# Sums of x, the first group's second half, quarter sums and stores of results moved in a kernel of sliding-window attention and Sinkhorn-routed experts

## The chip, the cores and the metric

The kernel runs on one core of one Trainium2 chip. The metric is the device time of one execution in microseconds (us). The engines are called as the profile calls them: PE (TensorE matmuls), PEld (its weight loads), DVE (VectorE), ACT (ScalarE), POOL (GpSimd) and SP (SyncE, which here only issues transfers). Each engine runs its own instructions in the order of the program and waits on semaphores for the others.

## The reference

Attention over 8 batches, 8 heads, 576 positions of 64, in a window of 128 back, with a bias that falls linearly with the distance. Its output, 4608 tokens of 512, is the input `x` of a mixture of 8 experts: all experts work on all tokens, and the routing weights come from 8 rounds of Sinkhorn normalisation over all tokens.

```python
def _attn_ref(q, k, v):
    ...
    mask = (rel >= 0) & (rel < window)
    scores = np.where(mask, scores + bias[None], -1000000000.0)
    ...
    return np.matmul(attn, v)

def _moe_ref(x, w_gate, w1, w2):
    ...
    P = np.exp(logits)
    for _ in range(8):
        P /= P.sum(1, keepdims=True) + 1e-09
        P /= P.sum(0, keepdims=True) + 1e-09
        P *= N / E
    out = np.zeros((N, D), dtype=np.float32)
    for e in range(E):
        h = np.maximum(x @ w1[e], 0.0)
        ye = h @ w2[e]
        out += P[:, e:e + 1] * ye
    return out
```

## The kernel before

The order of every engine's instructions is written out by hand in the program: what is called first is issued first.

**The attention stage** runs over 8 batches, each in 5 blocks of keys (`kb`, four of 128 and a tail of 64) and two halves of the heads (`u`). A step `(b, kb, u)` has a place in its batch, `at = 2 * kb + u`. A step issues the scores of the step ahead on PE (L412, L419), its exponentials on ACT (L430), the mask on DVE (L443), the products with v of the present step on PE (L468), and their normalisation on DVE (L478, L479). Around this stands what prepares the coming batches:

- `load_qk` (L271) loads q and k of batch b + 2 at `at == 3`, through SP's queue.
- `cast_qk` casts them to 16 bits in four parts: k on ACT (L289), q on DVE (L287). The first two parts of batch b + 2 are cast at places 8 and 9 of batch b, the others at places 0 and 1 of batch b + 1. On ACT the first of them stands ahead of the exponentials of batch b + 1.
- `turn_qk` (L301) turns q and k of batch b + 1 with two transposing transfers in SP's queue, at `at == 1`, for b = 2 to 6. `order_qk` (L312) brings them into order, k on POOL and q on DVE.
- `turn_x` writes the turned attention output into the tiles `xT`, from batch 3 on with a transposing transfer (L519).

**The filler** puts the dense products of experts 0 and 1 between these steps, so that PE has work while the softmax chain is under way: `l1` (L115, eight 128x512 products and a ReLU on ACT, L127) and `l2` (L137, eight matmuls into one bank, then `keep`). `keep` casts the result on DVE into a tile `yo` (L555); the tiles rotate through `YO` slots. The cast result isn't stored at once. It is appended to a list, and `store(left)` (L541) issues the stores of all but the last `left` of the list, in order, on SP's queue; `keep` calls `store(2)` ahead of its cast. A cast into a slot that is used again waits until the store from that slot has landed. The PSUM banks of the tag `pmm` are four, shared by the products of the filler, the attention and the units below; a bank is free when the cast or copy that reads it is done.

**The Sinkhorn rounds** follow, with filler between.

**The routed stage** handles experts 2 to 7. A unit is a group of 256 tokens and an expert, 108 units in order of group, `n` counts them. Most units make both products with seven partial products in place of eight (Strassen's scheme). This needs sums of quarters of the operands: for `x` the function `sums_x` (L909 to L911, three DVE instructions), for the first weights `quads_w1` (L933, four per expert; for expert 7 one of them is split in two, L931), for the second weights `sums_of` (L630, five per expert). The last two are put into a list `todo`, and `some(k)` issues the next k of them; `more_sums` says how many unit n issues near its beginning and at its end. Units of experts 6 and 7 of the first group (n = 4, 5) use plain products (`l1_bank`, L957), since their quarter sums aren't made yet.

In a seven-product unit, PE's banks go by letters: product A, a copy of A into B on ACT (L1138), product C, a copy of C into the tile `s5y` (L1142), more onto B, a copy of B into C (L1147), and so on. L1153 and L1159 are the two DVE additions that end the first layer's unit; the next product into bank B waits for L1153. `make_sums` (L995 to L997) adds up the hidden activations, and `product` (L1015) makes the second layer of the unit before, in between. When a group ends, `gather` (L1059) adds the banks into `acc` on DVE, which frees them for the next group.

`begin(g, e)` puts the stored results of experts 0 and 1 into `acc`: the first half L1031, the second L1035. They are loaded by `load_y` (L1025). For the first group the second half's load is issued at the end of unit 4, and `begin(g, 1)` stands near the beginning of unit 5, ahead of unit 5's `sums_x` for unit 6.

The passage between the stages runs so: x of the first two units is scaled and transposed (L887, L897), then the last filler products go in pieces, with some quarter sums after each:

```python
        got = filler.fill(0.9)
        some(int(got / L1_US + 0.5))
        got = filler.fill(0.9)
        sums_x(0)
        while got:
            some(int(got / L1_US + 0.5))
            got = filler.fill(0.9)
```

Of the kernel before, what the change touches and what calls it, by code (L numbers as in the profile page):

```python
# [14 lines left out]
def kernel(  # L15
# [18 lines left out]
    E = moe_w_gate.shape[1]  # L34
# [129 lines left out]
            yield 0, a  # L164

    L1_US, L2_US = 0.87, 1.74
    XPE, YO, XSB = 3, 6, 12
    CAST_AT = ((0, 1, 2, 3), (1, 2, 3, 4))

    class Filler:  # L170
# [58 lines left out]
    if True:  # L229
# [308 lines left out]
        def store(left=0):  # L538
            while len(stores) > left:
                e, blk, yo = stores.pop(0)  # L540
                nc.sync.dma_start(out=ysp[e, blk], in_=yo)  # L541
# [101 lines left out]
        def some(n):  # L643
            for _ in range(min(n, len(todo))):
                todo.pop(0)()
# [43 lines left out]
        for n, (b, kb, u) in enumerate(steps):  # L689
            nxt = steps[n + 1] if n + 1 < len(steps) else None  # L690
            at = 2 * kb + u
            left = ((10 - at) % 10 + 1) if b >= XPE else 10 - at + 9 * (at == 9)
            budget = filler.backlog() / (11 if (b, at) == (XPE, 0) else left)
            if b == 0:
                budget = 0.0
            if nxt:
                if nxt[0] < XPE and nxt[1:] == (RI - 2, 1):
                    turn_pe(nxt[0], 0, NDT)
                if nxt == (1, 0, 0):
                    filler.ready = RI  # L700
                    spin_alone(6)
                    for _ in range(NFT):
                        filler.take()
                    cast_qk(1, 0)
                    cast_qk(1, 1)
                    for j in range(NDT):
                        turn_pe(1, 1, j)
                        turn_pe(1, 0, j)
                        if j < 2:
                            cast_qk(1, j + 2, (1,))  # L710
                        filler.take()
                if nxt == (2, 0, 0):
                    filler.fill(8.5)
                    cast_qk(2, 0)
                    cast_qk(2, 1)
                    filler.fill(2.5)
                    for j in range(NDT):
                        turn_pe(2, 1, j)
                        turn_pe(2, 0, j)
                        if j < 2:  # L720
                            cast_qk(2, j + 2, (1,))
                        filler.fill(1.0)
                if n == 0:
                    scores(*nxt)
                elif nxt[2] == 0:
                    scores(*nxt)
                    scores(*nxt[:2], 1)
                exps(*nxt)
            got = filler.fill(1.0) if b else 0.0
            if nxt:  # L730
                masks(*nxt)
            values(b, kb, u)
            if n > 0 and u == 0 and by_pe(steps[n - 1][0]):
                turn_x(*steps[n - 1][:2])
            if u == 1 and n // 2 + NKB < B * NKB:
                cast_v(n // 2 + NKB)
            filler.fill(budget - got)
            if at == 0 and b > XPE:
                filler.ready = 4 * b
            if at < 8 and b < XPE:  # L740
                filler.ready = 4 * b + at // 2
            if at == 8 and b < XPE:
                filler.ready = 4 * b + 4
            if u == 1 and not by_pe(b):
                turn_x(b, kb)
            if u == 1:
                if kb == 1 and b > 0:
                    gates(4 * b - 4, 4 * b)
                if n // 2 + NKB + 1 < B * NKB:
                    load_v(n // 2 + NKB + 1)  # L750
            if b == 0 and at == 5:
                load_weights(1)
            if (b, at) == (1, 8):
                filler.allowed.add(1)
            if (b, at) == (1, 5):
                for j in (2, 3):
                    cast_qk(2, j, (0,), True)
            if (b, at) == (1, 2):
                filler.hold = False
            if (b, at) == (0, 9):  # L760
                load_qk(2, 2)
            if (b, at) == (0, 7):
                homes(1)
            if (b, at) == (1, 3):
                homes(2)
            if 1 <= b < B - 2 and at == 3:
                load_qk(b + 2)
            if XPE <= b + 1 < B - 1 and at >= 8:
                cast_qk(b + 2, at - 8)
            if XPE <= b + 1 < B:  # L770
                if at == 0 and b + 1 == XPE:
                    cast_qk(b + 1, 0)
                    cast_qk(b + 1, 1)
                if at < 2:
                    cast_qk(b + 1, at + 2)
                if at == 1:
                    turn_qk(b + 1)
                    order_qk(b + 1, 1, range(NDT))
                if at == 5:
                    turn_tail(b + 1)  # L780
                if at in (6, 7):
                    order_qk(b + 1, 0, range(2 * at - 12, 2 * at - 10))
            if b < B - 1 and at == (1 if b > 1 else 5) and b:
                load_tail(b + 1)
            if 10 * b + at >= 66:
                i = 10 * b + at - 66
                if i % 8 == 0:
                    home_last(2 + i // 8)
                (load_w2 if i % 8 < 4 else load_w1)(2 + i // 8, i % 4, 4)
            if (b, at) == (7, 0):  # L790
                todo += sums_of(2, *extras(2))
            if b == 7 and at >= 5:
                some(1)
# [302 lines left out]
        for e in range(2, 5):  # L1096
            todo += quads_w1(e)
        todo += quads_w1(5)
        got = filler.fill(0.9)
        some(int(got / L1_US + 0.5))  # L1100
        got = filler.fill(0.9)
        sums_x(0)
        while got:
            some(int(got / L1_US + 0.5))
            got = filler.fill(0.9)
        todo += sums_of(5, *extras(5))
        store()
# [2 lines left out]
        todo += sums_of(6, F1_6, w2f[:, 2], w2f[:, 3])  # L1110
        todo += sums_of(7, aux[:, 0], w2f[:, 0], w2f[:, 1]) + quads_w1(6) + quads_w1(7)
        more_sums = {0: (0, 1), 1: (2, 1), 2: (2, 1), 3: (2, 0), 4: (2, 1), 5: (2, 1), 6: (2, 0)}
        more_sums.update({n: (2, 0) for n in range(7, 11)})
        s5y = per.tile([P, 2, GT], FP32, name="s5y", tag="xTt", bufs=1)
        s5 = s5y[:, 0].rearrange("p (f t) -> p f t", f=NF2)
        y = s5y[:, 1].bitcast(FP16).rearrange("p (m d) -> p m d", m=2)
# [2 lines left out]
        for n in range(N):  # L1119
            g = units[n - 1][0]  # L1120
# [4 lines left out]
            some(more_sums.get(n, (0, 0))[0])  # L1125
            if done:
                gather(units[n - 2][0], 6, 7)
            if n > 0 and units[n - 1][1] == 6:
                begin(g, 1)
            y_first_half = n > 0 and units[n - 1][1] == (5 if g == groups[0] else 4)  # L1130
            if y_first_half:
# [1 line left out]
            if strassen(n):  # L1133
                new_h(n)
                pa = bank(n, "A")
                part(n, pa, "a11", B11, True)
                pb = bank(n, "B")
                nc.scalar.copy(out=pb, in_=pa)  # L1138
                product(n - 1, 3)
                pc = bank(n, "C")  # L1140
                part(n, pc, "s1", T1, True)
                nc.scalar.copy(out=s5, in_=pc)  # L1142
                product(n - 1, 4)
                if end:
                    gather(g, 3, 4)
                part(n, pb, "s2", T2)
                nc.scalar.copy(out=pc, in_=pb)  # L1147
                part(n, pa, "a12", B21)
                relu(n, 0, pa)
                scale_x(n + 2)  # L1150
                product(n - 1, 5, 2)
                part(n, pb, "s3", T3)
                nc.vector.tensor_tensor(out=h[n][:, 3], in0=pb, in1=s5, op=ALU.add)  # L1153
                relu(n, 3, h[n][:, 3])
                if done:
                    gather(units[n - 2][0], 1)
                part(n, pc, "s4", B22)
                turn_xs(n + 2)
                nc.vector.tensor_tensor(out=h[n][:, 1], in0=pc, in1=s5, op=ALU.add)  # L1159
                relu(n, 1, h[n][:, 1])  # L1160
                sums_x(n + 1)
                if end:
                    gather(g, 5, 2)
                product(n - 1, 6, 7)
                part(n, pb, "a22", T4)
                relu(n, 2, pb)
                product(n - 1, 1)
            else:
                pairs = ((3, 4), (5, 2), (6, 7), (1,))
                for i in range(4):  # L1170
                    l1_bank(n, i)
                    if i == 1:
                        scale_x(n + 2)
                    product(n - 1, *pairs[i])
                    if end and i in (0, 1):
                        gather(g, *pairs[i])
                turn_xs(n + 2)
                sums_x(n + 1)
            some(more_sums.get(n, (0, 0))[1])
            if done:  # L1180
                finish(units[n - 2][0])
# [42 lines left out]
```

## Time and profile before

| | us |
|---|---|
| median of 3 runs | 1018.19 (1016.83 to 1020.91) |
| the profiled execution | 1019.14 |
| its span, first to last instruction | 1017.4 |
| DVE busy | 754.7 |
| ACT busy | 728.9 |
| mean granted clock of PE | 0.998 |

The profile records one execution. Its views group instructions by source line, list them in order of time with the idle time of the engine before each and what ended that idle time, and sum busy times over stretches. A wait for several events is put down to the last of them. The attention stage takes up to about 280 us, the Sinkhorn rounds and the passage up to about 340, and the rest is the routed stage. The span starts at 0.

### The profile page before, as it was taken

Reading aid. Unit: us, or ns where it says so; the run is one execution under the profiler, and the core shown is the slowest. Engines: PE = TensorE matmul, PEld = TensorE weight load, DVE = VectorE, ACT = ScalarE, POOL = GpSimd, SP = SyncE. Lnnn points to the kernel's source line nnn. Section 1 sums busy time; section 2 is a strip of 40 time slices with the busy share of each in tenths; the row PEclk is TensorE's granted clock in tenths of the full one; section 3 lists DMA queues with packets and bytes.
Section 4 is the critical chain, followed back from the end, with each engine's and each line's share of the span. In section 5 each row is a group of like instructions: output and inputs, shape, how many; then the busy total and the mean of one; then the engine's idle time right before and its main releaser. Section 6 shows DMA issues by size and latency. Waiting matters only on the chain.

```text
span 1017.4 us, 27990 instructions
## 1 busy us (share of the span) xinstructions
PE 999.1 (98%) x11583; PEld 803.1 (79%) x11583; DVE 754.7 (74%) x1614; ACT 728.9 (72%) x1252; POOL 78.1 (8%) x143
## 2 busy tenths in 40 slices
PE   8999999999999999999999999999999999999998
PEld 5645444444444698999999999999999999999997
DVE  5837565655677979877877877887887887787787
ACT  7655554555333667888888888888888888888885
POOL 1213123315110000000000000000000000000000
PEclk9999999999999999999999999999999999999999
DMA  9998799889998223334333334334334333433461
GB/s 251 206 252 216 146 210 234 210 185 170 231 191 171 69 63 87 69 77 95 78 65 99 74 65 95 74 64 96 80 63 98 82 74 78 94 74 66 98 113 50
DMA packets 264431, 122.46 MB, mean 120 GB/s; under 512 B 201968, under 2 KB 255728, under 8 KB 264304
## 3 DMA queue, kind: packets, MB, share of 16 engines
q1 hardware_dynamic: 249568, 102.68, 44.3%
q0 software_dynamic: 14304, 17.84, 10.6%
q8 instruction: 90, 1.47, 0.6%
q14 instruction: 37, 0.30, 0.1%
q10 hardware_dynamic: 432, 0.16, 0.1%
HBM read 78.30 MB, written 23.59 MB: 100 GB/s over the span
## 4 chain that ended last, share of the span: by engine, by line
PE 86%; DVE 4%; DMA 4%; SPq 3%; issue 1%; ACT 1%; POOL 0%; DVEq 0%; POOLq 0%; ACTq 0%
PE psM L1015 31%; PE psB L978 14%; PE psh L115 9%; PE psA L978 9%; PE psC L978 9%; PE psy L137 9%; PE psN L468 1%; DMA ysp<-yo 1%; PE psS L412 1%; SPq L271 1%; DMA v<-in_v_dram 1%; DMA k<-in_k_dram 1%; PE psh L957 1%; SPq L374 1%; DVE yo L555 1%
## 5 line engine op out<-in xcount | busy, mean ns | idle before, releaser
L1015 PEld LDWEIGHTS <-hs 128*128 128x128 f16 x2996 | 271.1, 98 | 23.6 <-issue 1.6
L1015 PE MATMUL psM<-w2l,hs 128*128 128x256 f16 x1440 | 186.6, 273 | 1.0 <-DVE acc L1059 1.0
L978 PEld LDWEIGHTS <-w1l 128*128 128x128 f16 x2848 | 181.3, 98 | 5.8 <-issue 1.6
L991 ACT ACTIVATE hs<-hs 128x512 f16<-128x512 f16 x212 | 130.5, 631 | 35.0 <-DVE hs L1153 25.0
L978 PEld LDWEIGHTS <-s 128*128 128x128 f16 x2136 | 141.6, 98 | 7.7 <-issue 1.7
L1153 DVE TENSOR_TENSOR hs<-psB,s5y 128x512 f16<-128x512 f32 x106 | 73.3, 692 | 98.2 <-ACT xs L887 91.6
L115 PE MATMUL psh<-xT,w1t 128*128 128x512 f16 (+1 forms) x608 | 140.3, 371 | 3.3 <-DVE yo L555 2.1
L127 ACT ACTIVATE hT<-psh 128x512 f16<-128x512 f32 (+1 forms) x144 | 83.2, 587 | 82.2 <-PE psh L115 82.0
L887 ACT ACTIVATE xs<-xtok,L_sb 128x512 f16<-128x512 f16 x204 | 136.5, 723 | 2.7 <-DMA xset<-xs 2.7
L137 PE MATMUL psy<-w2t,hT 128*128 128x512 f16 x576 | 135.0, 379 | 0.0
L1015 PE MATMUL psM<-more,hs 128*128 128x256 f16 x864 | 129.4, 273 | 0.0
L978 PE MATMUL psB<-xset,s 128*128 128x128 f16 x1424 | 108.5, 219 | 0.4 <-ACT psC L1147 0.4
L978 PE MATMUL psA<-xset,w1l 128*128 128x128 f16 x1424 | 108.5, 219 | 0.0
L137 PEld LDWEIGHTS <-hT 128*128 128x128 f16 x576 | 53.5, 98 | 60.3 <-issue 1.9
L115 PEld LDWEIGHTS <-w1t 128*128 128x128 f16 x608 | 55.0, 99 | 56.5 <-issue 8.1
L430 ACT ACTIVATE pt<-psS 128x1024 f16<-128x1024 f32 (+2 forms) x80 | 67.7, 852 | 43.5 <-PE psS L419 20.0
L555 DVE CAST yo<-psy 128x512 f16<-128x512 f32 x68 | 46.7, 690 | 69.8 <-PE psy L137 53.8
L995 DVE TENSOR_TENSOR hs<-hs 128x1024 f16<-128x1024 f16 x107 | 74.0, 691 | 21.3 <-ACT hs L991 19.3
L1147 ACT COPY psC<-psB 128x512 f32<-128x512 f32 x106 | 60.5, 571 | 37.7 <-PE psB L978 37.7
L1142 ACT COPY s5y<-psC 128x512 f32<-128x512 f32 x106 | 62.2, 587 | 22.3 <-PE psC L978 22.2
L1138 ACT COPY psB<-psA 128x512 f32<-128x512 f32 x106 | 61.0, 575 | 23.4 <-PE psA L978 23.3
L1059 DVE TENSOR_TENSOR acc<-acc,psM 128x256 f32<-128x256 f32 (+1 forms) x162 | 73.9, 503 | 0.3
(121 smaller groups left out, 1385.3 us busy)
## 6 DMA issues: line engine op xcount, KB each, us to landing
s5y<-ysp SPq DMA_DIRECT2D x36, 256.0 KB, 3.0
ysp<-yo SPq DMA_DIRECT2D x68, 128.0 KB, 3.6
v<-in_v_dram SPq DMA_DIRECT2D x32, 256.0 KB, 4.7
out_dram<-acc SPq DMA_DIRECT2D x31, 256.0 KB, 2.6
q<-in_q_dram SPq DMA_DIRECT2D x5, 1024.0 KB, 7.4
k<-in_k_dram SPq DMA_DIRECT2D x5, 1024.0 KB, 9.9
xtok<-xd SPq DMA_DIRECT2D x34, 128.0 KB, 2.3
w2t<-in_moe_w_dram POOLq DMA_DIRECT2D x4, 1024.0 KB, 10.5
```

The source lines that it names most:

```text
L115: nc.tensor.matmul(out=ps[:, 0:nt], lhsT=w1ts[e][:, dt, P * ft : P * ft + P], rhs=xT[:, at : at + nb, dt, :], start=(dt == 0), stop=(dt == ...
L127: nc.scalar.activation(out=st["hT"][:, ft, 0:nt], in_=ps[:, 0:nt], func=AF.Relu)
L137: nc.tensor.matmul(out=ps, lhsT=st["hT"][:, ft, P * ms : P * ms + P], rhs=w2ts[e][:, ft, :], start=(ft == 0), stop=(ft == NFT - 1),)
L430: nc.scalar.activation(out=pt[0:nk, :, 0 : nk + nn], in_=ps[0:nk, :, :, 0 : nk + nn].rearrange("p a y n -> p (a y) n"), func=AF.Exp, scale ...
L887: nc.scalar.mul(out=xs[2 * (n % 2) + m], in_=xtok[m], mul=P_sb[:, blk, e : e + 1])
L978: nc.tensor.matmul(out=ps[:, j, :], lhsT=q[k][:, P * j : P * j + P], rhs=xset[n % 2][:, x, P * k : P * k + P], start=(start and j == 0 and ...
L991: nc.scalar.activation(out=h[n][:, slot], in_=src, func=AF.Relu)
L995: nc.vector.tensor_tensor(out=t[:, 4:6], in0=t[:, 0:2], in1=t[:, 2:4], op=ALU.add)
L1015: nc.tensor.matmul(out=Ms[bk][:, half, :], lhsT=h[n][:, LEFT[m], f, :], rhs=W2L[e][RIGHT[m]][:, f, :], start=(e == 2 and f == 0 and half = ...
L1059: nc.vector.tensor_tensor(out=a, in0=a, in1=p2, op=op)
L1142: nc.scalar.copy(out=s5, in_=pc)
L1153: nc.vector.tensor_tensor(out=h[n][:, 3], in0=pb, in1=s5, op=ALU.add)
```

## The change

Four things move, and one count grows:

1. `YO` is 7 in place of 6: one more slot for the cast results.
2. `store(1)` is called ahead of `turn_qk` in batches 2 to 6: all stores on the list but the last are issued ahead of the two transposes. On SP's queue these are two stores each time, which stood behind the transposes before.
3. `sums_x(0)` stands after the eighth piece of the last filler work, not after the second. On DVE it moves behind eight instructions that make quarter sums and one cast of a result.
4. The first group's `begin(g, 1)` moves from near the beginning of unit 5 to its end, behind `sums_x(6)`.
5. The quarter sums of experts 6 and 7 that unit 7 issued (two) are issued from unit 8 on, some at the ends of units 8 and 9.

The instructions of PE, ACT and POOL, and their order, stay as they are.

```diff
-    XPE, YO, XSB = 3, 6, 12
+    XPE, YO, XSB = 3, 7, 12
...
                 if at == 1:
+                    store(1)
                     turn_qk(b + 1)
...
         todo += quads_w1(5)
+        pieces = 0
         got = filler.fill(0.9)
-        some(int(got / L1_US + 0.5))
-        got = filler.fill(0.9)
-        sums_x(0)
         while got:
             some(int(got / L1_US + 0.5))
+            pieces += 1
+            if pieces == 8:
+                sums_x(0)
             got = filler.fill(0.9)
...
-        more_sums.update({n: (2, 0) for n in range(7, 11)})
+        more_sums.update({8: (2, 1), 9: (2, 1), 10: (2, 0)})
...
-            if n > 0 and units[n - 1][1] == 6:
+            if n > 0 and units[n - 1][1] == 6 and g != groups[0]:
                 begin(g, 1)
...
                 sums_x(n + 1)
+            if n == E - 3:
+                begin(g, 1)
             some(more_sums.get(n, (0, 0))[1])
```

## The prediction

> **What bounds the kernel now.** First the page's head, then the busy time in stretches of 25 us (columns: stretch and its length, then busy time and instructions of PE, PEld, DVE, ACT, POOL, the granted clock, DMA share, GB/s).
>
> ```profile
> span 1017.4 us, 27990 instructions
> PE 999.1 (98%) x11583; PEld 803.1 (79%) x11583; DVE 754.7 (74%) x1614; ACT 728.9 (72%) x1252; POOL 78.1 (8%) x143
> ```
>
> ```profile
> 125.00:150.00 25.00, 22.91 (x164) 10.87 (x160) 15.16 (x35) 13.77 (x23) 7.95 (x13) 0.93 0.88 212
> 325.00:350.00 25.00, 22.11 (x189) 14.10 (x188) 20.14 (x37) 14.46 (x26) 0.00 (x0) 1.00 0.28 70
> 375.00:400.00 25.00, 23.16 (x308) 21.53 (x306) 23.87 (x49) 17.46 (x32) 0.00 (x0) 1.00 0.31 76
> ```
>
> TensorE bounds the kernel: 18.3 us of the span is all that it idles. The change leaves TensorE's instructions and their order as they are, so it can win only idle time of PE and time at a lowered clock. The three stretches shown idle 2.1, 2.9 and 1.8 us, and in the first the mean clock is 0.93, worth up to 25 x 0.07 = 1.75 us. These are the three places that the change touches, so 8.5 us is a ceiling.
>
> **Place A, the entry into the first seven-product unit.** VectorE and PE, from the timeline (start, length, engine, line; the idle time before, in brackets):
>
> ```profile
> 331.40 0.43 DVE L909 TENSOR_TENSOR xset<-xset 128x512 f16<-128x512 f16 x1 [3.21 <-DMA xset<-xset]
> 332.25 7.07 PE L137 MATMUL psy<-w2t,hT 128*128 128x512 f16 x32
> 332.47 1.28 DVE L933 TENSOR_TENSOR s<-w1l 128x1024 f16<-128x1024 f16 x2
> 336.20 0.69 DVE L555 CAST yo<-psy 128x512 f16<-128x512 f32 x1
> 340.67 0.61 PE L978 MATMUL psC<-xset,s 128*128 128x128 f16 x8 [0.90 <-DVE yo L555]
> 343.66 0.68 DVE L1153 TENSOR_TENSOR hs<-psB,s5y 128x512 f16<-128x512 f32 x1
> 344.40 0.61 PE L978 MATMUL psB<-xset,w1l 128*128 128x128 f16 x8 [0.79 <-DVE hs L1153]
> ```
>
> VectorE stands 3.21 us for the transposes of x, is then late with four casts of finished sums (yo), and PE waits for their banks and for L1153. The change puts the three sums of x (332.47 - 331.40 = 1.07 us) behind eight quarter sums and one cast. The 3.21 us then fill with quarter sums. What is late next is the data of the first yo cast: it needs the first 8 of PE's 32 matmuls, 332.25 + 7.07/4 = 334.0, while the old queue reached it at 336.20. From 334.0 on the queue is the old one with 1.07 us of sums inside, so every later VectorE step moves by 336.20 - 334.03 - 1.07 = 1.10 us: the cast that frees psC's bank, and L1153. PE's gap at 340.67 closes, and its restart at 344.40, set by L1153, moves by 1.10. I take **-1.1 us**. The ends: 0.4 (the copies on ScalarE between the products set the pace instead) and 0.90 + 0.79 = 1.7 (both gaps gone). The moved sums end near 337.0 and are first read by psC, near 339.6: 2.6 us of cover; without it PE would pay their delay one for one. Up to the cast that frees psC's bank, one cast and two quarter sums queue behind them; the 1.10 already holds that.
>
> **Place B, the end of the first group.**
>
> ```profile
> 369.76 2.50 SPq L897 DMA_TRANSPOSE xset<-xs  x2
> 375.29 1.42 DVE L1035 SCALAR_TENSOR_TENSOR acc<-s5y,L_sb,acc 128x512 f32<-128x512 f16 x2 [1.98 <-DMA s5y<-ysp]
> 376.62 0.42 DVE L909 TENSOR_TENSOR xset<-xset 128x512 f16<-128x512 f16 x1
> 377.61 0.68 DVE L630 TENSOR_TENSOR w2f<-w2t 128x1024 f16<-128x1024 f16 x1
> 378.34 0.60 PE L1015 MATMUL psM<-w2f,hs 128*128 128x256 f16 x4 [0.34 <-DVE w2f L630]
> 383.01 0.61 PE L978 MATMUL psB<-xset,w1l 128*128 128x128 f16 x8 [0.54 <-DVE hs L1153]
> 387.45 1.28 DVE L933 TENSOR_TENSOR aux<-w1l 128x1024 f16<-128x1024 f16 x2
> 388.65 0.74 DVE L1059 TENSOR_TENSOR acc<-acc,psM 128x256 f32<-128x256 f32 x2
> 389.45 1.03 PE L1015 MATMUL psM<-w2l,hs 128*128 128x256 f16 x8 [0.97 <-DVE acc L1059]
> ```
>
> L1035 (the second half's begin) waits 1.98 us for its load, with the sums of x queued behind it. The change runs the sums first. Their transposes were issued at 369.76, ahead of that load in the same queue, so they should have landed by then. So 377.61 - 376.62 = 0.99 us of work goes into the wait, and the quarter sum w2f, then L1153, come 1.0 us earlier. That removes the gap of 0.34 and most of that of 0.54. The gap of 0.97 falls because the two quarter sums at 387.45 (388.65 - 387.45 = 1.20) no longer stand ahead of the gather at 388.65 that frees PE's bank. The idle times sum to 1.85. The first two are worth at most the 1.0 by which VectorE moves. For the third I add the 0.17 by which a group of 8 (0.61 busy) outlasts its share of the pace (32 matmuls of four times the width in 7.07: 0.055 each, 0.44 for 8): 1.1. I take **-2.1 us**, ends 1.0 (only the third) and 2.3 (all three with their tails).
>
> The quarter sums that leave unit 7 land in units 8 to 10, one more at the end of 8 (0.60) and two halves at the end of 9:
>
> ```profile
> 397.93 0.69 DVE L995 TENSOR_TENSOR hs<-hs 128x1024 f16<-128x1024 f16 x1 [0.20 <-ACT hs L991]
> 401.66 0.68 DVE L1153 TENSOR_TENSOR hs<-psB,s5y 128x512 f16<-128x512 f32 x1
> 402.69 0.61 PE L978 MATMUL psB<-xset,w1l 128*128 128x128 f16 x8
> ```
>
> In unit 9 L1153 ends at 402.34 and PE needs it at 402.69: 0.35 us of cover, against about 0.3 of delay (the 0.60, less a 0.2 us wait that it fills and a shorter first half). I cost it at nothing; uncovered it is 0.3 us, once.
>
> **Place C, the stores ahead of the transposes of q and k.** The timeline of batch 3, and the clock in three windows of 2 us:
>
> ```profile
> 117.77 6.27 SPq L301 DMA_TRANSPOSE qk<-c  x2
> 125.44 1.64 SPq L541 DMA_DIRECT2D ysp<-yo  x3
> 128.46 0.69 DVE L555 CAST yo<-psy 128x512 f16<-128x512 f32 x1 [4.22 <-DMA ysp<-yo]
> 129.20 1.86 PE L115 MATMUL psh<-xT,w1t 128*128 128x512 f16 x4 [2.09 <-DVE yo L555]
> ```
>
> ```profile
> 128.00:130.00 2.00, 0.80 (x2) 0.25 (x2) 1.54 (x3) 0.45 (x1) 2.00 (x3) 0.80 0.71 184
> 130.00:132.00 2.00, 2.00 (x13) 1.03 (x12) 1.33 (x5) 0.60 (x1) 0.45 (x2) 0.50 0.88 179
> 132.00:134.00 2.00, 2.00 (x15) 0.76 (x13) 1.62 (x3) 0.72 (x2) 1.53 (x3) 0.85 0.85 282
> ```
>
> The stores of results stand on SP's queue behind 6.27 us of transposes; a cast waits 4.22 us for its slot, PE 2.09 for the cast, and then runs at half clock for 0.8 + 2.0 + 0.6 = 3.4 us, a loss of 1.7. Either edit alone removes this wait: two stores go ahead, and with seven slots a cast waits for the store seven before it instead of six. So 3.8 us vanish at 129.2. But PE has the next wait in sight:
>
> ```profile
> 130.25 0.89 SPq L271 DMA_DIRECT2D k<-in_k_dram  x1
> 140.85 0.62 ACT L289 CAST c<-k 128x512 f16<-128x512 f32 x1 [4.89 <-DMA k<-in_k_dram]
> 142.42 0.69 DVE L443 TENSOR_TENSOR pt<-pt,mask 128x1024 f16<-128x1024 f16 x1
> 142.03 1.90 PE L137 MATMUL psy<-w2t,hT 128*128 128x512 f16 x8
> 143.77 0.29 PE L468 MATMUL psN<-v,pt 128*128 128x65 f16 x4
> 141.81 1.19 SPq L519 DMA_TRANSPOSE xT<-xsb  x1
> 144.53 1.04 PE L115 MATMUL psh<-xT,w1t 128*128 128x512 f16 x4
> ```
>
> ```profile
> DMA to landing us min/median/max: 2.3/2.3/2.3
> ```
>
> ScalarE waits for the load of k. The exponentials of batch 4 are queued behind that cast, then the mask, done at 142.42 + 0.69 = 143.11, and PE's psN needs it. PE reaches psN at 143.77 today, so only 0.66 us of the 3.8 is free. k is issued at 130.25 with the same transfers ahead of it as before, in another order, so its landing should stand. Next, L115 at 144.53 reads a transposed block issued at 141.81; the last line, for that transpose, gives 2.3 us to land: 144.1. So the gain ends at 0.4 us, and PE stands about 3.1 us ahead of 143.1 instead of 2.09 at 129.2. If the clock halves for 3.4 us again from there, psN and the scores (144.53 - 143.77 = 0.76) take 1.52, to 144.66, and of the 1.89 us left at half clock 0.95 is lost: behind by 0.13 + 0.95 = 1.1. So C lies between -0.4 and +1.1. One dip cannot tell where in a stall the halving begins, and what passes within the stall costs nothing, so I take the middle, **+0.3 us**.
>
> [...]
>
> The other four transposes are delayed by two stores (about 1.1 us by 1.64 for three). PE shows no idle time for them, so they cost nothing; uncovered, 1.1 us each.
>
> **The sum** is -1.1 - 2.1 + 0.3 = **-2.9 us**. The profiled execution took 1019.14 (span 1017.4 and 1.7 around it) and would take 1016.2. It lies 0.95 above the median of the three runs, 1018.19, so the median becomes **1015.3**. With the ends (A 0.4 to 1.7, B 1.0 to 2.3, C +1.1 to -0.4) that is 1013.8 to 1017.9.
>
> **The rivals.**
> 1. *The wait for k does not hold.* The load lands some 3 us earlier, as two stores no longer stand just ahead of it, or ScalarE's late start is made up; place C gives its whole 3.8. Against it: as many transfers precede k as before. For it: the DMA engines are not full at 130 (share 0.71 to 0.88). Sum -1.1 - 2.1 - 3.8 = -7.0: **1011.2**.
> 2. *The load of k slips.* Transposes behind two stores run on into the loads of q and k, and PE waits at psN for each microsecond that k is later. From a slip of 2.1 us (A and B's 3.2 less the half clock's 1.1) the kernel is slower than before. With 3.5: 3.5 + 1.1 - 3.2 = +1.4, **1019.6**. Against it: stores go in front, but none is added.
> 3. *The change doesn't do what it says at A and B.* ScalarE's copies take over at A and the load of y is still ahead at B: 0.4 + 1.0 won, 0.3 lost, **1017.1**.
>
> **How the numbers follow.** Forecast 0.57, first rival 0.28, second 0.07, third 0.08. Half a per cent, about what a measurement of this kernel can tell from no change, is 5.1 us. Faster by more (under 1013.1): the first rival and 0.05 of the forecast, 0.33. Slower by more (over 1023.3) needs a slip beyond 7 us, half of the second rival: 0.04. The rest, 0.63, is within. The range reaches to the first rival and past the third: 1011.0 to 1018.6.
>
> **What would show it.** PE's idle at 340.67 gone and that before psB smaller in time; none of the gaps of 0.34 and 0.97 in the first group's end; no wait of yo for ysp, and full clock near 129. The test of the middle step is a new idle time of PE near 140 to 143, released by DVE's mask, with ScalarE waiting some 8.6 us for k: if it is missing, rival 1 holds. If k lands after 142, rival 2. A gap that moves to another line at A or B is rival 3.

## The result, and the profile after

| | before | after |
|---|---|---|
| median of 21 runs each, side by side, us | 1017.66 (1015.25 to 1021.77) | 1014.38 (1011.73 to 1018.19) |
| ratio, with its 95% interval | | 0.996 (0.995 to 0.997) |
| the profiled execution, us | 1019.14 | 1018.19 |
| its span, us | 1017.4 | 1016.4 |

The change makes the kernel 3.3 us faster, a third of a per cent. The forecast was 2.9 us. The profiled execution of after is the longest of its 21 runs, 3.8 us above their median, so the two spans do not show the gain, and the traces have to be compared stage by stage. The page's head, and busy time in the three stretches that the prediction read (same columns):

```profile
span 1016.4 us, 27989 instructions
PE 1000.7 (98%) x11583; PEld 804.7 (79%) x11583; DVE 758.9 (75%) x1614; ACT 727.7 (72%) x1252; POOL 80.7 (8%) x143
```

```profile
125.00:150.00 25.00, 22.60 (x169) 10.37 (x166) 16.83 (x37) 11.84 (x20) 8.67 (x13) 0.93 0.89 211
325.00:350.00 25.00, 22.88 (x181) 13.73 (x179) 19.35 (x35) 14.18 (x26) 0.00 (x0) 1.00 0.37 82
375.00:400.00 25.00, 24.99 (x328) 23.41 (x326) 23.61 (x49) 19.60 (x35) 0.00 (x0) 1.00 0.43 86
```

The last stretch idled 1.84 us before and 0.01 now. The first idled 2.09 us before and 2.40 now, and its clock is 0.93 again: something took the place of the stall that went.

**How the stages are compared.** PE runs the same 11583 matmuls in the same order in both kernels, so the start of the same matmul can be subtracted. The psB restart behind L1153, for one, started at 344.40 before; it starts at 345.73 now (its line is L1155 there), 1.33 us later. Such a difference holds all that came earlier, so only its change over a stage counts (minus is won):

| over the stage (times of before) | after minus before at its ends, us | won or lost, us |
|---|---|---|
| start-up, up to 126 | 0 to +2.27 | +2.3 |
| place C, 126 to 185 | +2.27 to +2.00 | -0.3 |
| place A, 331 to 350 | +2.29 to +1.33 | -1.0 |
| place B, 370 to 391 | +1.33 to -0.82 | -2.15 |
| the rest | | +0.1 |

The difference at 126 arises ahead of the first stores that move (near 85 us): from 70 to 126 us it stays within 0.01. Experiments 2, 3, 10 and 11 below, which leave these 126 us as in before, stand there between -0.6 and +2.6, so executions differ in the start-up by themselves. The sum of the places, -3.4, is near the 3.3 us between the medians.

**Place A.** VectorE and PE, from the timeline of after (start, length, engine, line; in brackets the idle time before):

```profile
336.47 0.69 DVE L555 CAST yo<-psy 128x512 f16<-128x512 f32 x1 [2.54 <-PE psy L137]
338.40 0.42 DVE L910 TENSOR_TENSOR xset<-xset 128x512 f16<-128x512 f16 x1
339.25 0.29 DVE L912 TENSOR_TENSOR xset<-xset 128x256 f16<-128x256 f16 x1
342.00 0.61 PE L979 MATMUL psC<-xset,s 128*128 128x128 f16 x8
344.07 0.61 PE L979 MATMUL psB<-xset,s 128*128 128x128 f16 x8 [0.26 <-ACT psC L1149]
345.73 0.61 PE L979 MATMUL psB<-xset,w1l 128*128 128x128 f16 x8 [0.61 <-DVE hs L1155]
```

VectorE no longer stands for x's transposes. It now waits 2.54 us for the data of the first cast, as the prediction said it would. psC starts without idle time (0.90 before), and its sums were ready at 339.54.

**Place B.** VectorE:

```profile
374.88 0.43 DVE L910 TENSOR_TENSOR xset<-xset 128x512 f16<-128x512 f16 x1 [0.24 <-DMA xset<-xs]
376.58 1.41 DVE L1036 SCALAR_TENSOR_TENSOR acc<-s5y,L_sb,acc 128x512 f32<-128x512 f16 x2 [0.62 <-DMA s5y<-ysp]
377.91 0.68 DVE L630 TENSOR_TENSOR w2f<-w2t 128x1024 f16<-128x1024 f16 x1
```

The sums of x fill the wait: 0.24 + 0.62 us are left of 1.98.

**Place C.** First VectorE's waits of casts for their slots, before and after (us in total, times, longest), then the timeline of after around the load of k, and what a transpose at 143.29 took to land:

```profile
DVE yo L555 <- DMA ysp<-yo: 13.5, 5, 4.2
```

```profile
DVE yo L555 <- DMA ysp<-yo: 1.7, 1, 1.7
```

```profile
142.31 0.62 ACT L289 CAST c<-k 128x512 f16<-128x512 f32 x1 [7.99 <-DMA k<-in_k_dram]
142.83 1.02 ACT L430 ACTIVATE pt<-psS 128x1024 f16<-128x1024 f32 x1
143.29 1.19 SPq L519 DMA_TRANSPOSE xT<-xsb  x1
143.88 0.69 DVE L443 TENSOR_TENSOR pt<-pt,mask 128x1024 f16<-128x1024 f16 x1 [3.17 <-ACT pt L430]
144.63 0.30 PE L468 MATMUL psN<-v,pt 128*128 128x65 f16 x4 [2.33 <-DVE pt L443]
145.66 1.16 PE L115 MATMUL psh<-xT,w1t 128*128 128x512 f16 x4
...
DMA to landing us min/median/max: 2.3/2.3/2.3
```

The old stall at 129.20 and its half clock are gone: by 140 us PE has won 3.9 us on its place at 126. Then it stands 2.33 us for the mask, the mask for the exponentials, and these for a cast that waited 7.99 us for k (4.89 before). L115 starts at 145.66, right after the block that it reads landed, 143.29 + 2.3 = 145.6. And the clock halves once more behind this stall. Two windows of 3.41 us (busy times, then the clock, DMA share and GB/s):

```profile
143.03:146.44 3.41, 1.73 (x16) 0.81 (x16) 2.52 (x6) 3.41 (x5) 0.67 (x2) 1.00 0.84 198
146.44:149.85 3.41, 3.41 (x13) 1.25 (x12) 2.55 (x8) 1.47 (x3) 0.94 (x2) 0.50 0.61 175
```

So 3.9 us are won, and by 150 us 4.5 are given back. Near 180, where PE stood 0.65 us for the mask before and does not in after, 0.8 are won again.

### The profile page after: what moved, and what is told of

Read it like the earlier page. It is cut to its first block, busy times and chain, and to the rows that moved or that the text cites. A ratio compares the mean times of both kernels' runs of the same rounds, so it can differ in the third digit from the quotient of the medians.

```text
span 1016.4 us, 27989 instructions
## 1 busy us (share of the span) xinstructions
PE 1000.7 (98%) x11583; PEld 804.7 (79%) x11583; DVE 758.9 (75%) x1614; ACT 727.7 (72%) x1252; POOL 80.7 (8%) x143
## 3 DMA queue, kind: packets, MB, share of 16 engines
q0 software_dynamic: 14304, 17.84, 10.5%
q8 instruction: 90, 1.47, 0.6%
## 4 chain that ended last, share of the span: by engine, by line
PE 92%; DMA 3%; DVE 2%; ACT 1%; SPq 1%; issue 1%; POOL 0%; ACTq 0%; DVEq 0%; POOLq 0%
PE psM L1016 32%; PE psB L979 14%; PE psh L115 11%; PE psy L137 11%; PE psA L979 9%; PE psC L979 9%; PE psN L468 2%; PE psS L412 1%; DMA v<-in_v_dram 1%; DMA k<-in_k_dram 1%; PE psh L958 1%; PE psX L506 0%; DMA qk<-c 0%; DVE yo L555 0%; DMA ident<-ident_c 0%
## 5 line engine op out<-in xcount | busy, mean ns | idle before, releaser
L1155 DVE TENSOR_TENSOR hs<-psB,s5y 128x512 f16<-128x512 f32 x106 | 73.4, 692 | 97.1 <-ACT xs L888 87.1
L115 PE MATMUL psh<-xT,w1t 128*128 128x512 f16 (+1 forms) x608 | 140.2, 371 | 1.5 <-ACT hT L127 1.5
L137 PE MATMUL psy<-w2t,hT 128*128 128x512 f16 x576 | 135.0, 379 | 0.0
L137 PEld LDWEIGHTS <-hT 128*128 128x128 f16 x576 | 53.5, 98 | 60.3 <-issue 1.9
L115 PEld LDWEIGHTS <-w1t 128*128 128x128 f16 x608 | 55.1, 99 | 54.9 <-issue 6.0
L443 DVE TENSOR_TENSOR pt<-pt,mask 128x1024 f16<-128x1024 f16 (+2 forms) x80 | 53.0, 662 | 35.1 <-ACT pt L430 35.0
```

The costliest lines, as they stand in the source:

```text
L115: nc.tensor.matmul(out=ps[:, 0:nt], lhsT=w1ts[e][:, dt, P * ft : P * ft + P], rhs=xT[:, at : at + nb, dt, :], start=(dt == 0), stop=(dt == ...
L137: nc.tensor.matmul(out=ps, lhsT=st["hT"][:, ft, P * ms : P * ms + P], rhs=w2ts[e][:, ft, :], start=(ft == 0), stop=(ft == NFT - 1),)
```

## The experiments

Ratios are to the kernel before on the same chip, with 95% intervals. "C", "A" and "B" are the time lost (plus) or won (minus), in us, over the stages of the table above. They come from one profiled execution each, compared with the one of before.

**1. Slots and stores alone** (place C)

```diff
-    XPE, YO, XSB = 3, 6, 12
+    XPE, YO, XSB = 3, 7, 12
                 if at == 1:
+                    store(1)
                     turn_qk(b + 1)
```

> The kernel before with seven slots and the two stores ahead of the transposes of q and k alone (place C). Theory: PE's idle of 2.09 us near 129 and the half clock behind it go, a new idle of PE of 2 to 3 us comes some 14 us later at the psN that waits for the mask, behind ScalarE's wait for k (8 us in place of 4.9), with a half clock of 3.4 us behind it; time between -0.8 and +1 us of before, ratio 0.999 to 1.001. Rival, the wait removed is won: 3.8 us less, ratio 0.996, and the other two places give nothing. The gap of 0.65 near 180 goes by the trace of the changed kernel: that is 0.7 of gain inside the first figure.

Measured: ratio 0.9998 (0.9981 to 1.0016), medians 1019.84 and 1018.74. C -1.8, A +0.7, B 0. The stall moves as in after, but the half clock that was expected behind it does not come here. The timeline, then two windows on the grid that this execution's last clock change gives:

```profile
141.66 0.30 PE L468 MATMUL psN<-v,pt 128*128 128x65 f16 x4 [2.32 <-DVE pt L443]
```

```profile
137.67:141.08 3.41, 1.66 (x8) 0.58 (x6) 0.24 (x2) 1.75 (x3) 0.00 (x0) 1.00 1.24 265
141.08:144.49 3.41, 2.76 (x23) 1.24 (x24) 3.34 (x10) 3.25 (x5) 0.67 (x2) 1.00 0.68 186
```

At A, with the sums of x still early, psC waited longer than in before, as x's transposes landed later:

```profile
329.65 0.42 DVE L910 TENSOR_TENSOR xset<-xset 128x512 f16<-128x512 f16 x1 [3.96 <-DMA xset<-xset]
338.91 0.61 PE L979 MATMUL psC<-xset,s 128*128 128x128 f16 x8 [1.61 <-DVE yo L555]
```

That wait was 3.21 before, and psC's gap 0.90: the wait grew by 0.75 and the gap by 0.71. What follows: the stores and slots by themselves change nothing that 12 runs can tell.

**2. Sums of x later, alone** (place A)

```diff
+        pieces = 0
         got = filler.fill(0.9)
-        some(int(got / L1_US + 0.5))
-        got = filler.fill(0.9)
-        sums_x(0)
         while got:
             some(int(got / L1_US + 0.5))
+            pieces += 1
+            if pieces == 8:
+                sums_x(0)
             got = filler.fill(0.9)
```

> The kernel before with the sums of x for the first seven-product unit behind the eighth piece alone (place A). Theory: 0.9 to 1.1 us less, ratio 0.999; VectorE's idle of 3.2 us ahead of L909 gone, PE's gap ahead of psC gone, gaps of 0.2 to 0.4 and 0.6 left where 0.39 and 0.79 stood. Rival, the copies on ScalarE take over: 0.4 us or less. The gaps near 129, 378, 383 and 389 stay as they are.

Measured: ratio 0.9993 (0.9974 to 1.0011). A -0.96, B 0, C -0.7. The psC gap is gone and 0.60 is left at psB:

```profile
343.76 0.61 PE L978 MATMUL psB<-xset,w1l 128*128 128x128 f16 x8 [0.60 <-DVE hs L1154]
```

What follows: 1 us of the prediction's 1.1, the same as in after. The interval alone would not have told it; the matmul starts do.

**3. The first group alone** (place B)

```diff
-        more_sums.update({n: (2, 0) for n in range(7, 11)})
+        more_sums.update({8: (2, 1), 9: (2, 1), 10: (2, 0)})
...
-            if n > 0 and units[n - 1][1] == 6:
+            if n > 0 and units[n - 1][1] == 6 and g != groups[0]:
                 begin(g, 1)
...
+            if n == E - 3:
+                begin(g, 1)
```

> The kernel before with the first group's second half at the end of unit 5 and the quarter sums moved from unit 7 to units 8 to 10 (place B). Theory: the three gaps of 0.34, 0.54 and 0.97 go, 2.15 us less, ratio 0.998, and no gap opens in units 8 to 10. Rival, the load of y still comes after the sums and holds VectorE: only the last gap goes, 1.0 us less.

Measured: ratio 0.9967 (0.9953 to 0.9981), B -2.05, A 0. Most of the change's gain is here.

**4. The change, with q and k loaded a place earlier**

```diff
-            if 1 <= b < B - 2 and at == 3:
+            if 1 <= b < B - 2 and at == (2 if b > 1 else 3):
                 load_qk(b + 2)
```

> The changed kernel with the loads of q and k of batch b + 2 issued one place earlier, so that they stand ahead of one store, a transpose of x, a store of x and a load of v on the queue (batches 2 to 5). Theory, PE's idle near 143 is the wait for k: k lands some 3 us earlier, the idle of 2.3 us shrinks under 1 us, the half clock behind it goes, and the time falls by 2 to 4 us against the changed kernel, ratio to before 0.993 to 0.994. Rival, the next wait stands right behind (the transpose of x that L115 reads, or v): under 1 us less, ratio 0.996. Second rival, what is delayed on the queue (x, v) costs PE more than k gives: slower than the changed kernel.

Measured: ratio 0.9984 (0.9969 to 0.9999), C +1.0, A and B as in after. PE no longer stands behind the wait for k (psN starts at 141.57 without idle time). But the loads now stand ahead of x's transposes in the queue, and PE waits longer for those:

```profile
146.40 1.12 PE L115 MATMUL psh<-xT,w1t 128*128 128x512 f16 x4 [3.99 <-DMA xT<-xsb]
```

What follows: k is not the only wall near 143. A block of `xT` stands behind it.

**5. The change, without the cast of k ahead of batch 4's exponentials**

```diff
-            if XPE <= b + 1 < B - 1 and at >= 8:
+            if XPE == b + 1 and at >= 8:
                 cast_qk(b + 2, at - 8)
             if XPE <= b + 1 < B:
-                if at == 0 and b + 1 == XPE:
+                if at == 0 and b + 1 != XPE + 1:
                     cast_qk(b + 1, 0)
                     cast_qk(b + 1, 1)
```

> The change, with the first two casts of a batch's q and k put from places 8 and 9 of the batch before to place 0 of the batch itself, from the fifth batch on: ScalarE has no cast to wait with ahead of batch 4's first exponentials. My theory is that two walls stand one behind the other near 143 us, the load of k and the transposed block that L115 reads next, which landed at 145.60: ScalarE's wait of 7.99 us for k and TensorE's stall of 2.33 us at psN go, TensorE comes to L115 some 2 us earlier and waits there about as long; the ratio stays within 0.001 of the change's, near 0.996. Rival: k alone is the wall, the 2.33 us and, where it comes, the half clock behind them are won: ratio 0.992 to 0.994.

Measured: ratio 0.9956 (0.9941 to 0.9971), C +0.2, median 1015.29 beside 1015.32 for the change on the same chip. The timeline, the block's time to land, and two windows:

```profile
141.05 1.66 ACT L289 CAST c<-k 128x512 f16<-128x512 f32 x3 [2.95 <-DMA k<-in_k_dram]
142.03 1.19 SPq L519 DMA_TRANSPOSE xT<-xsb  x1
144.39 1.41 PE L115 MATMUL psh<-xT,w1t 128*128 128x512 f16 x4 [3.23 <-DMA xT<-xsb]
...
DMA to landing us min/median/max: 2.3/2.3/2.3
```

```profile
141.48:144.89 3.41, 0.50 (x3) 0.36 (x4) 3.33 (x8) 2.15 (x4) 0.67 (x2) 1.00 0.95 222
144.89:148.30 3.41, 3.41 (x13) 1.30 (x12) 1.49 (x4) 1.14 (x2) 0.71 (x2) 0.50 0.54 158
```

The stall at psN is gone, and PE stands 3.23 us at L115 until 142.03 + 2.3 = 144.3. Two walls, one behind the other: taking one away brings PE to the other.

**6. The change, with the loads of q and k later in all batches from the fourth on**

```diff
-            if 1 <= b < B - 2 and at == 3:
+            if 1 <= b < B - 2 and at == (7 if b >= XPE else 3):
                 load_qk(b + 2)
-            if XPE <= b + 1 < B - 1 and at >= 8:
+            if XPE == b + 1 and at >= 8:
                 cast_qk(b + 2, at - 8)
             if XPE <= b + 1 < B:
-                if at == 0 and b + 1 == XPE:
+                p = at if b <= XPE else at - 2
+                if p == 0 and b != XPE:
                     cast_qk(b + 1, 0)
                     cast_qk(b + 1, 1)
-                if at < 2:
-                    cast_qk(b + 1, at + 2)
-                if at == 1:
+                if 0 <= p < 2:
+                    cast_qk(b + 1, p + 2)
+                if p == 1:
                     store(1)
```

> The change, with the loads of q and k from the sixth batch on at place 7, not 3, the casts at places 2 and 3 of the next batch and the transposes behind them at place 3: the two issues of the loads (2.8 us of the DMA queue from 131 us on) come behind the transposes of batch 3, and no cast stands ahead of batch 4's first exponentials. Theory of two walls: both move, the block that L115 reads lands near 142.5, no stall over 0.5 us between 138 and 148 us, and 2 to 4 us are won on the change: ratio 0.992 to 0.9945, a median near 1012. Rival: the queue passes the lateness on, the casts in batch 4 wait for k, landing near 151 us, ahead of its next exponentials, and a stall of 2 us or more comes back before 185 us: ratio 0.996 or more.

Measured: ratio 1.0091 (1.0066 to 1.0116). Both walls are gone (C -3.5, no stall between 138 and 148), and the rival's lateness comes later and larger, 13 us between 185 and 260:

```profile
190.98 0.88 PE L137 MATMUL psy<-w2t,hT 128*128 128x512 f16 x2 [3.64 <-ACT hT L127]
229.90 1.09 PE L137 MATMUL psy<-w2t,hT 128*128 128x512 f16 x2 [3.02 <-ACT hT L127]
...
187.86 1.66 ACT L289 CAST c<-k 128x512 f16<-128x512 f32 x3 [3.80 <-DMA k<-in_k_dram]
```

The casts wait for k once more, now on ScalarE ahead of the filler's `hT`. Half clock follows the two stalls: eight matmuls of L137 take 3.57 us at 192.10 and 2.77 at 231.25, and 1.89 at 195.74. In batch 3 the later load fits, in batches 4 and 5 it does not.

**7. The change again**, beside 5 and 6 on their chip, with no edit.

> The change itself, beside the two others of this call on the same chip: ratio 0.995 to 0.997, as before. Theory: a stall of 2 to 2.5 us at psN near 144 us again, since it hangs on the DMA queue and the landing of k; whether half clock follows it is open (3.4 us of it in the first profile of the change, none where the stores and slots were alone). Rival: the stall was of that one execution: then it is under 1 us here.

Measured: ratio 0.997 (0.9956 to 0.9984), medians 1015.32 and 1018.72. C +0.3, A -0.96, B -2.0. The stall is there again, and the half clock behind it:

```profile
141.41 0.62 ACT L289 CAST c<-k 128x512 f16<-128x512 f32 x1 [8.52 <-DMA k<-in_k_dram]
143.73 0.30 PE L468 MATMUL psN<-v,pt 128*128 128x65 f16 x4 [2.87 <-DVE pt L443]
...
142.00:145.42 3.42, 1.61 (x16) 0.81 (x16) 2.40 (x6) 3.42 (x6) 0.67 (x2) 1.00 0.88 206
145.42:148.83 3.41, 3.41 (x13) 1.33 (x12) 2.62 (x8) 1.59 (x3) 0.66 (x2) 0.50 0.56 158
```

**8 and 12. The earlier stores alone, and the seventh slot alone**, one execution each

```diff
+                    store(1)
                     turn_qk(b + 1)
```

> The kernel before with the stores ahead of the turns alone, six slots. Theory: the stores are what is late, so bringing them ahead of the two transposes is enough: VectorE's waits of results for their slots fall from 13.5 us in sum to under 5, and the 2.09 us stall near 129 is gone. Rival: the slot is what counts: a stall of over 1 us at a result's conversion stays between 125 and 135 us. In both, the stall near 143 behind k stays, at 2 to 3 us, and the time is within 2 us of before.

```diff
-    XPE, YO, XSB = 3, 6, 12
+    XPE, YO, XSB = 3, 7, 12
```

> The kernel before with a seventh slot for results alone, the stores where they were. Theory: the stores are late behind the transposes of q and k by more than one slot's worth (a result comes every 2 to 3 us, the two transposes hold the queue for 5 to 10), so a wait for ysp<-yo stays at a result's conversion between 125 and 135 us, and TensorE's stall there shrinks but stays over 0.3 us. Rival: one slot is enough, and no stall over 0.2 us stands between 125 and 135 us.

Measured: 1022.31 and 1016.20 us (before: median 1018.72 and 1020.03 on their chips). In both the stall near 129 is gone and the one near 143 is there, first with the stores, then with the slot:

```profile
145.73 0.30 PE L468 MATMUL psN<-v,pt 128*128 128x65 f16 x4 [1.47 <-DVE pt L443]
```

```profile
140.71 0.30 PE L468 MATMUL psN<-v,pt 128*128 128x65 f16 x4 [1.70 <-DVE pt L443]
```

VectorE's waits for slots fall to 5.1 us with the stores alone (under 5 was expected), and with the slot alone none is left. So I was wrong on experiment 12: one slot is enough. On experiment 8 the stall near 143 came out shorter than the 2 to 3 us expected, and the time 3.6 us above the median of before, not within 2. Either edit does at place C what both do (C -1.8 and -2.2, with no half clock in either: four matmuls of L115 behind the stall take 1.04 and 1.02 us, where at half clock in before, at 129.20, they took 1.86). Of the 6 us between the two times 5.2 are not theirs: at 126 us the executions stand at +4.2 and -1.0 against before.

**9. The change, with the later load in batch 3 alone.** Batch 4 loads one place later than in the change, the others where they did. As in experiment 5, no cast stands ahead of the exponentials of batch 4 or a later one. The edit is that of 6, with

```diff
-            if 1 <= b < B - 2 and at == 3:
+            if 1 <= b < B - 2 and at == {XPE: 7, XPE + 1: 4}.get(b, 3):
...
+                p = at - 2 * (b == XPE + 1)
```

> The change, with the later load for the sixth batch alone: its q and k loaded at place 7 of batch 3 and cast and turned at places 2 and 3 of batch 4; batch 4 loads at place 4, the others at 3 as in the change, and from the seventh batch on the first casts stand at place 0 of the batch itself. Theory: the wall near 143 us lifts as it did with all loads later (no stall over 0.5 us between 138 and 148) and the stalls behind hT near 191 and 230 us, which came from the loads at place 7 of batches 4 and 5, do not come: 2 to 3 us won on the change, ratio 0.992 to 0.995. Rival: the queue of the loads is full in batch 4 too, its lateness comes back as a stall of over 2 us between 150 and 200 us, and the ratio is 0.996 or more.

Measured: ratio 0.9936 (0.9917 to 0.9955), medians 1013.05 (6 runs) and 1020.03. C -3.2, A -1.0, B -2.0. A window over both walls, the one stall that is left, and its cause on ScalarE:

```profile
138.00:148.00 10.00, 10.00 (x76) 4.91 (x75) 7.93 (x20) 3.32 (x4) 3.48 (x9) 1.00 0.66 164
...
157.13 0.88 PE L137 MATMUL psy<-w2t,hT 128*128 128x512 f16 x2 [0.98 <-ACT hT L127]
...
154.01 1.66 ACT L289 CAST c<-k 128x512 f16<-128x512 f32 x3 [1.14 <-DMA k<-in_k_dram]
```

PE is busy through both walls at full clock, and the 3.9 us won at 129 stay won but for this stall. The version beats before by 6.5 us by its ratio; against the change, whose intervals are 0.995 to 0.997 and 0.9956 to 0.9984, the lead is some 3 us, but the change did not run beside it, and its interval overlaps the first. Experiment 5 moved the casts without the load and won nothing at C, so the moved casts alone don't do it.

**10 and 11. The second half's begin alone, and the quarter sums alone** (place B), one execution each. The edits are the last two and the first of experiment 3.

> The kernel before with the first group's second half moved to the unit's end alone. Theory: the gap of 0.97 us at the first psM after the gather, behind acc, near 390 us goes, and with it the half at 383 that waited for the same engine; the gap at w2f near 378 stays, as it belongs to the quarter sums: 0.9 to 1.6 us less between 375 and 395 us. Rival: with the quarter sums still there, the conversions stay late and one of the gaps of 0.5 to 1 us comes back by 395 us: under 0.6 us won.

> The kernel before with fewer quarter sums in the first group's units 7 to 10 alone. Theory: the gap of 0.34 to 0.43 us at w2f near 378 goes and that at psB behind hs near 383 shrinks; the 0.97 us behind acc near 390 stays: 0.3 to 1.1 us less between 375 and 395 us. Rival: the quarter sums were what made acc late too, and the whole 2.1 us go with them.

Measured: B -0.9 and -1.1. The gaps that are left, first with the begin moved, then with the quarter sums moved:

```profile
388.49 1.03 PE L1015 MATMUL psM<-w2l,hs 128*128 128x256 f16 x8 [0.96 <-DVE acc L1059]
```

```profile
379.20 0.60 PE L1015 MATMUL psM<-w2f,hs 128*128 128x256 f16 x4 [0.32 <-DVE w2f L630]
383.86 0.61 PE L978 MATMUL psB<-xset,w1l 128*128 128x128 f16 x8 [0.53 <-DVE hs L1153]
```

Both expectations had the gaps the wrong way round. The begin removes the first two gaps and the quarter sums the third, just as the prediction had split them, 1.0 and 1.1.

## Why the prediction was right

**Place A: right.** -1.1 was forecast, and three executions gave -0.96. The step that carries it, that VectorE would next be late only for its first cast's data, is the 2.54 us wait at 336.47. psC's gap went and that before psB shrank from 0.79 to 0.61. With the sums early, the lateness of x's transposes goes straight to psC (experiment 1: 0.75 more wait, 0.71 more gap); with the sums late it is covered. Place A lost 0.7, 0.7 and 0.3 us in experiments 1, 8 and 12, where slot or stores moved and the sums did not, and nothing in experiments 3, 10 and 11, which move neither. The prediction did not count this.

**Place B: right, part by part.** -2.1 was forecast, with 1.0 for the begin and 1.1 for the quarter sums; measured were -2.15 and -2.0 in the change, and -0.9 and -1.1 apart. The sums' transposes had not quite landed as the prediction held: VectorE still waits 0.24 us for them at 374.88. The quarter sums that went to units 8 to 10 cost nothing that shows, as costed.

**Place C: right in mechanism, near in size by luck in part.** Forecast was +0.3 between -0.4 and +1.1, and -0.3 and +0.3 were measured. Its steps in these two executions: the old wait goes (13.5 us of slot waits to 1.7); ScalarE waits for k (8.6 said, 7.99 and 8.52 measured); PE stands at psN for the mask (3.1 said, 2.33 and 2.87); the clock halves again (3.4 us said, 3.41 from 146.44 and from 145.42). k landed 10.2 us after its issue at 132.05, at 142.25, against 130.25 + 10.5 = 140.75 before. This execution was 2.27 us late already, so against its own start-up k came 0.8 us earlier, where the prediction let it stand, and the stall is that much shorter. The second wall, the block that L115 reads, was named there and is shown by experiments 4 and 5. That the middle of the range was met is luck in part. The 0.8 us won near 180 (0.7 in experiment 7) are not in the prediction: up to 150 us C was +0.6 and +1.1, between the forecast and its upper end. And where no half clock followed (experiment 1), C was -1.8, below the range.

**The rivals.** The first, a k that comes early enough for the whole 3.8 us, fell on the chip: the wait for k grew by 3 us or more. Experiment 9 comes near to what it priced, by moving the load as well: 1011.2 was its time, with 7.0 us won in sum, and 6.5 were measured. The second needed a slip of 2.1 us, and there was none. Its sign, k landing after 142, did come (142.25), but by the late start-up alone. The third fell with A and B.

**What it did not say.** Whether the half clock follows a stall is not settled by the stall's length. Stalls of 2.33 and 2.87 us were followed by it, those of 2.32, 1.47 and 1.70 (experiments 1, 8, 12) were not. The old stall at 129 behaves so too: with its code untouched it was 1.80 us in experiment 11 and kept full clock (1.02 us for the first four matmuls behind it, 1.86 in before), and C came out at -2.0 with nothing changed there. So the 1.7 us that the prediction counted as won at 129 are not lost in every execution of before. In 28 of the 56 runs of before beside experiments 1 to 8 the mean granted clock was 1.0, and so it was in 18 of the 33 runs of the change: half clock comes about as often with the change as without. Beside experiments 9 to 12, where the change did not run, it was 1.0 in 2 of 11 runs of before. The clock is not all of it: in experiment 10 the old stall (1.76 us) kept full clock too, but C was -0.3. Of the 1.5 us won by 140 us, 0.8 went by 150, from a short wait of psN for the mask on (0.22 us), and 0.4 near 180, where psN stood 1.08 us for the mask. In sum, C lies between -2.2 and +0.3 in an execution whether both edits are in, or one, or none. The runs give no gain to place C that can be told from zero; A and B, -3.1 us together, are 0.997 of the time.

## What to carry to other kernels

A stall ahead of a wait for a transfer is cover for that transfer. Before costing its removal, look some 20 us down the same engine for the next instruction that stands on a landing that the edit does not bring forward, and for the one behind that: here the gain stopped at two walls, one behind the other (at 143.77 and 144.53 in before, where the stall stood at 129.20), and was kept only when the load itself moved. Small edits at different places are told apart by subtracting the starts of the same matmul, where medians of a dozen runs can't.

## What the runs showed of the hardware

**In these traces the half clock starts and ends on a grid.** All stretches whose ends are shown here are 3.41 us long (in the start-up of experiment 9 half clock goes on past the window of 43.44 to 46.85: at 46.76 four matmuls of L351 take 1.09 us, at 17.96 they take 0.63). In after they start at a whole number of such windows from each other, at 13.32, 23.56 and 146.44, 3 and 36 windows apart. After the start-up, the idle time in the window before each tells a little more in these executions than the length of the stall: PE idled 2.09 us in the window ahead of the old half clock at 129.20, 3.41 - 1.73 = 1.68 in after, 3.42 - 1.61 = 1.81 in experiment 7 and 2.91 in experiment 5. In experiment 1 the boundary at 141.08, placed by that execution's last clock change, cut the stall of 2.32, and 1.75 fell into the one window: the clock stayed, 1.00 in both windows. So did it with 1.76 in experiment 10, whose stall at the old place was 1.76 us long:

```profile
125.30:128.71 3.41, 1.65 (x16) 0.78 (x15) 1.20 (x2) 1.90 (x3) 3.41 (x4) 1.00 0.74 206
128.71:132.12 3.41, 3.25 (x29) 1.46 (x28) 3.01 (x8) 1.56 (x3) 1.50 (x4) 1.00 0.88 231
```

About half a window of idle time, 1.7 to 1.8 us, is my estimate, from these numbers, of where it tips in these executions; the two outcomes overlap there (1.68 halved, 1.76 did not). And idle time is not all: in the start-up of after, 1.22 us in the window ahead of 13.32 were followed by half clock (0.50 from 13.32 to 16.74). Why stays open.

**The start-up differs by itself.** At 126 us, ahead of the three places, the profiled executions stand between -1.0 us (experiment 12) and +5.9 us (experiment 9) against before. What differs are stalls such as these, in after and in experiment 9:

```profile
23.40 0.44 PE L468 MATMUL psN<-v,pt 128*128 128x65 f16 x7 [1.90 <-POOL v L385]
```

```profile
44.19 1.87 PE L137 MATMUL psy<-w2t,hT 128*128 128x512 f16 x4 [1.94 <-DMA w2t<-in_moe_w_dram]
```

That is twice what the change wins, so a single time of a kernel says nothing of it. What makes these late in one execution and not in another stays open.
